# Four edits to a one-core attention and expert kernel: the place of a loop that is not entered, of the state products, of the last counting products and of the first expert's row read

## The chip, the cores and the metric

The kernel runs on one core of a Trainium2 chip. The metric is the device time of one execution in microseconds (us), taken as the median of several runs. A core has five engines that each follow a program of their own and wait for one another through semaphores: PE (matrix products), DVE (vector), ACT (scalar functions), POOL (general, and here the issuer of the indirect transfers) and SP (here the issuer of the plain transfers).

## The reference

Three steps follow one another on 3072 tokens of 384 numbers.

```python
for t in range(768):            # gated linear attention, 4 batches x 8 heads, head size 48
    state = alpha[:, :, t, :, None] * state + k_t (outer) v_t
    y[:, :, t] = q_t @ state
x = y, heads side by side       # 3072 x 384
xn = x / rms(x) * rms_g         # first feed-forward layer, width 1536
x = (silu(xn @ w_gate) * (xn @ w_val)) @ w_out
e_idx = argmax(x @ gate)        # one of 8 experts for each token, width 1024
out[mask_e] = weight * (relu(x[mask_e] @ w1[e]) @ w2[e])
```

## The kernel before, in words

Tokens are handled in 24 tiles of 128 for the attention and in groups of three tiles (384 tokens) for the first layer. Large products are made from operands split into a high and a low part, three products for one.

**Attention.** `stages(t)` gives five steps for a tile t: the scores (tile `ps_s`), a transposition of k (`ps_k`, copied to `kn`), the output (`outp`, tile `ps_y`), the state's new part (`state`, tile `ps_st`: 16 products of `v` and `kn`, 64x48 each) and the transposed, normalised output (`ps_x`). All five take their PSUM tile from one rotating set. The main loop over groups g has 36 slots n in a group; each slot issues nine products of 128x384 of the first layer (tiles `ps_g`, `ps_v`, `ps_o`), and at set counts one attention step is put between two slots. So `ps_y` and `ps_st` of a tile stand in two different slots.

**Routing.** `route_a` and `route_b` of a group find each token's expert. Six small products (tile `ps_r`, with the constants `tri_b` and `ones_b`) count the tokens of each expert ahead of a token; DVE makes positions of them (`rk`, `pos`), and POOL scatters the rows `R` to a DRAM buffer `bucket` that has a region for each expert.

**Experts.** The experts are taken in the order of their counts. `parts` lists the units of work u: u=0 and u=1 are the two halves, 256 rows each, of the leading expert, which is known six groups early or so (`pick_first`); u=2 to 8 are the other seven experts, known only when the last group is counted (`pick_rest`, which also has SP load 21 addresses in all into registers, line 915). `load_rows` reads a unit's rows from `bucket` (tile `er`, queue of SP), `prep_rows` transposes them (`ps_t`, then `x2a` or `x`), `e_h(u, j)` makes a slice of the hidden layer (`ps_h`, then `h` on ACT and DVE), `e_o` multiplies it on (`ps_b`), `e_fin` scales the result and has POOL scatter it to the output (`out_dram`). `load_w1` and `load_w2` read the weights in pieces (tile `st`, queue of SP); ACT, DVE and POOL split them into the two parts.

**Surplus loop.** Rows beyond an expert's place in this scheme would be handled by a loop over `nblk` blocks at the end of the program (lines 1251 to 1323). On these inputs `nblk` is 0, so its body is not run, but each engine has to load the number (line 1223), wait for its own earlier work and jump over it. After it come the closing instructions of the program (line 1353).

**What sets the order.** Each engine runs its instructions strictly in the program's order. That order comes from a scheduler which simulates the kernel and may move what the code writes; where `strict[0]` is set and in `seq(...)` the order as written is kept. The mark `keep_in_program_order` does the same for one instruction.

Of the kernel before, what the change touches and what calls it, by code (L numbers as in the profile page):

```python
# [8 lines left out]
F32 = mybir.dt.float32  # L9
# [36 lines left out]
    'XO': 2,  # L46
    'STRICT': 4,
# [7 lines left out]
def gla_glu_moe_kernel(  # L55
# [16 lines left out]
    nc = tc.nc  # L72
# [771 lines left out]
    att_stream = (st for t in range(GT, NTILE) for st in stages(t))  # L844
# [180 lines left out]
    def e_h(u, j):  # L1025
        p, _, r, n = parts[u]
        xh, xl = x2[u]
        ps = psE.tile([P, r * n], F32, tag="h", name="ps_h", bufs=2)
        mm3(ps, *(w_[:, :, j * P:j * P + P] for w_ in we[p][0:2]), xh, xl)
        hh = act.tile([P, 2, r * n], F32R, tag="xl" if j % 2 else "xh", name="h2")  # L1030
        nc.scalar.activation(hh[:, 0, :], ps, AF.Relu)  # L1031
        nc.vector.scalar_tensor_tensor(out=hh[:, 1, :], in0=ps, scalar=0.0, in1=f(hh[:, 0, :]),  # L1032
                                       op0=ALU.max, op1=ALU.subtract)
        h2[u, j] = hh
# [32 lines left out]
    for g in range(2, NG):  # L1067
# [15 lines left out]
        for n in range(3 * KF):  # L1083
# [14 lines left out]
            if last:  # L1098
# [6 lines left out]
                if n == 30:  # L1105
                    load_rows(0, er0)
                if n >= 33:
                    prep_rows(0, n - 33)
# [21 lines left out]
    route_b(NG - 1)  # L1130
    pick_rest()
# [37 lines left out]

    lag = []  # L1170
# [24 lines left out]
    load_rows(1, ers[1])  # L1195
    load_next(1)
    weight_step()
# [3 lines left out]
    for u in range(U):  # L1201
        for j in range(KF2):
# [10 lines left out]
            elif j > 1 and u < U - 1:  # L1213
                pop_o()
            if u and j == 0 and u + 1 < U:
# [14 lines left out]
        if u >= 1 and u + 1 < U:  # L1230
            while ready or pw:
                weight_step()
            if parts[u + 1][0] + 1 < E:
                addresses(parts[u + 1][0] + 1)
                load_next(parts[u + 1][0] + 1)
    u = U - 1
# [4 lines left out]

    psE.release()
    psM.release()
    xp.release()
    wpool.release()


    with ExitStack() as ov:
        op_ = ov.enter_context(tc.tile_pool(name="op", bufs=1, side="right", reuse_waits="tile"))
        pp = ov.enter_context(tc.tile_pool(name="pp", bufs=2, space=PSUM))  # L1250
        with tc.For_i(0, nblk, 1):
            def sm(nm, w=1, dt=F32):
                return op_.tile([P, w], dt, tag=nm, name=nm)
            V = nc.vector
            ge = sm("ge", E)
            V.tensor_scalar(out=ge, in0=cb, scalar1=obk[:, 0:1], scalar2=None, op0=ALU.is_le)
            ef = sm("ef")
            V.tensor_reduce(out=ef, in_=ge, op=ALU.add, axis=AX.X)
            oh = sm("ohx", E)
            V.tensor_scalar(out=oh, in0=io8[:, 0, :], scalar1=ef[:, 0:1], scalar2=None, op0=ALU.is_equal)  # L1260
            V.tensor_tensor(out=ge, in0=oh, in1=cnt[:, 0, :], op=ALU.mult)
            ne = sm("ne")
            V.tensor_reduce(out=ne, in_=ge, op=ALU.add, axis=AX.X)
            V.tensor_tensor(out=ge, in0=oh, in1=cbx, op=ALU.mult)
            sl = sm("sl")
            V.tensor_reduce(out=sl, in_=ge, op=ALU.add, axis=AX.X)
            V.tensor_tensor(out=sl, in0=obk, in1=sl, op=ALU.subtract)
            V.tensor_tensor(out=ge, in0=oh, in1=capE[:, :, 0], op=ALU.mult)
            ce = sm("ce")
            V.tensor_reduce(out=ce, in_=ge, op=ALU.add, axis=AX.X)  # L1270
            V.scalar_tensor_tensor(out=sl, in0=sl, scalar=float(P), in1=ce, op0=ALU.mult, op1=ALU.add)
            V.tensor_tensor(out=sl, in0=sl, in1=pid[:, 0:1], op=ALU.add)
            rw = sm("rw")
            V.scalar_tensor_tensor(out=rw, in0=ef, scalar=float(REG), in1=sl, op0=ALU.mult, op1=ALU.add)
            ri = sm("ri", 1, I32)
            V.tensor_copy(ri, rw)
            V.tensor_tensor(out=sl, in0=sl, in1=ne, op=ALU.is_lt)
            V.scalar_tensor_tensor(out=rw, in0=sl, scalar=FAR, in1=rw, op0=ALU.mult, op1=ALU.add)
            zi = sm("zi", 1, I32)
            V.tensor_copy(zi, rw)  # L1280
            nc.gpsimd.indirect_dma_start(out=bucket[:, :], out_offset=OFF(ap=zi[:, 0:1], axis=0),
                                         in_=zrow[:, 0, :], in_offset=None,
                                         bounds_check=E * REG - 1, oob_is_err=False)
            r0 = nc.values_load(ri[0:1, 0:1], engines=[mybir.EngineType.SP], min_val=0, max_val=E * REG - P)
            wi = sm("wi", KD + KF2, I32)
            wf = sm("wf", KD + KF2)
            e3 = sm("e3", 2)
            V.tensor_scalar(out=e3[:, 0:1], in0=ef, scalar1=float(DM), scalar2=None, op0=ALU.mult)
            V.tensor_scalar(out=e3[:, 1:2], in0=ef, scalar1=float(F2), scalar2=None, op0=ALU.mult)
            V.tensor_scalar(out=wf[:, 0:KD], in0=pid[:, 1:1 + KD], scalar1=e3[:, 0:1], scalar2=None, op0=ALU.add)  # L1290
            V.tensor_scalar(out=wf[:, KD:], in0=pid[:, 1 + KD:], scalar1=e3[:, 1:2], scalar2=None, op0=ALU.add)
            V.tensor_copy(wi, wf)
            xr = sm("xr", RW)
            nc.sync.dma_start(xr[:, :], bucket[bass.ds(r0, P), :])
            wa = op_.tile([P, KD, F2], F32, tag="wa", name="wa")
            wb = op_.tile([P, KF2, DM], F32, tag="wb", name="wb")
            for i in range(KD):
                nc.gpsimd.indirect_dma_start(out=wa[:, i, :], out_offset=None,
                                             in_=w1.rearrange("e k n -> (e k) n"),
                                             in_offset=OFF(ap=wi[:, i:i + 1], axis=0))  # L1300
            for i in range(KF2):
                nc.gpsimd.indirect_dma_start(out=wb[:, i, :], out_offset=None,
                                             in_=w2.rearrange("e k n -> (e k) n"),
                                             in_offset=OFF(ap=wi[:, KD + i:KD + i + 1], axis=0))
            pt = pp.tile([P, KD, P], F32, tag="pt", name="ptx")
            for i in range(KD):
                nc.tensor.transpose(pt[:, i, :], xr[:, i * P:i * P + P], ident)
            xo = op_.tile([P, KD, P], F32, tag="xo", name="xo")
            V.tensor_copy(xo, pt)
            po = pp.tile([P, DM], F32, tag="po", name="po")  # L1310
            for j in range(KF2):
                ph = pp.tile([P, P], F32, tag="ph", name="ph")
                for i in range(KD):
                    nc.tensor.matmul(ph, lhsT=wa[:, i, j * P:j * P + P], rhs=xo[:, i, :],
                                     start=(i == 0), stop=(i == KD - 1))
                ht = op_.tile([P, P], F32, tag="ht", name="ht", bufs=2)
                nc.scalar.activation(ht, ph, AF.Relu)
# [40 lines left out]
```

## Time and profile before

| what | value |
|---|---|
| median of 3 runs | 868.49 us (866.66 to 868.85) |
| profiled execution, its own time | 865.15 us |
| its span in the trace | 863.4 us |
| PE busy | 840.6 us, 97% |
| DVE, ACT, POOL busy | 57%, 38%, 16% |
| PE's share of the chain that ended last | 79% |
| granted clock of PE over the span | 0.996 |

The profiled execution is one run under the profiler; 1.75 us of its own time lie outside its span. The busy share is a mean over the whole span. It says which engine has the most work, and not whether a given wait costs time: for that the stretches in which PE is not busy have to be looked at one by one.

### The profile page before, as it was taken

How to read it: one execution, taken by the hardware profiler on the slowest of the kernel's cores; microseconds unless marked ns; L12 is line 12 of the kernel's file. 1: busy time of each engine (PE TensorE's matmuls, PEld its weight loads, DVE VectorE, ACT ScalarE, POOL GpSimd, SP SyncE). 2: the span in 40 equal slices, each digit the busy share in tenths (PEclk: the TensorE clock that was granted, in tenths of full speed). 3: DMA queues.
4: the chain of work that ended last, by engine and by line, in shares of the span. 5: the costliest groups of instructions: out<-in, count | busy, mean ns of one | idle time of the engine just before them, and what ended most of it. 6: DMA issues, size and time to landing. Idle time of an engine off the chain costs nothing.

```text
span 863.4 us, 15649 instructions
## 1 busy us (share of the span) xinstructions
PE 840.6 (97%) x6036; PEld 806.6 (93%) x6036; DVE 491.0 (57%) x1111; ACT 324.7 (38%) x705; POOL 142.2 (16%) x204
## 2 busy tenths in 40 slices
PE   7999999999999999999999999999999999999994
PEld 5899989999999999999999999999998999999994
DVE  7998988577765655765655632343534343444320
ACT  2655543333323332333433332333235343345431
POOL 2100000001100100100010010013124242434331
PEclk9999999999999999999999999999999999999998
DMA  9964555852322222222232000041065165256510
GB/s 192 205 164 147 177 128 140 213 138 80 97 60 54 63 49 60 75 74 52 52 88 60 10 29 1 2 130 63 16 203 196 37 210 169 72 165 202 185 39 24
DMA packets 120268, 88.96 MB, mean 103 GB/s; under 512 B 55291, under 2 KB 115324, under 8 KB 120192
## 3 DMA queue, kind: packets, MB, share of 16 engines
q1 hardware_dynamic: 115728, 78.46, 34.5%
q0 software_dynamic: 4464, 9.48, 3.1%
q8 instruction: 48, 0.79, 0.4%
q14 instruction: 28, 0.23, 0.1%
HBM read 72.11 MB, written 16.07 MB: 102 GB/s over the span
## 4 chain that ended last, share of the span: by engine, by line
PE 79%; DVE 7%; issue 5%; DMA 4%; POOL 2%; SPq 1%; ACT 1%; POOLq 0%; DVEq 0%; ACTq 0%
PE ps_o L638 17%; PE ps_v L604 16%; PE ps_g L604 16%; PE ps_b L1047 9%; PE ps_h L604 9%; PE ps_s L425 3%; DMA st<-in_moe_w_dram 3%; PE ps_y L460 2%; PE ps_y L456 2%; PE ps_st L481 1%; SPq L915 1%; PE ps_k L445 1%; PE ps_x L502 1%; PE ps_t L1011 1%; POOL out_dram L1063 1%
## 5 line engine op out<-in xcount | busy, mean ns | idle before, releaser
L615 DVE TENSOR_TENSOR tt<-tt,ps_v 128x384 f32<-128x384 f32 x96 | 52.9, 551 | 119.8 <-PE ps_v L604 116.8
L618 ACT ACTIVATE hh<-tt 128x384 fp32r<-128x384 f32 x96 | 50.3, 524 | 125.2 <-DVE tt L615 119.5
L596 ACT ACTIVATE tt<-ps_g 128x384 f32<-128x384 f32 x96 | 47.1, 490 | 130.4 <-PE ps_g L604 127.3
L624 DVE TENSOR_TENSOR hl<-tt,hh 128x384 fp32r<-128x384 f32 x96 | 54.4, 566 | 27.5 <-ACT hh L618 27.3
L1032 DVE SCALAR_TENSOR_TENSOR h<-ps_h,h 128x256 fp32r<-128x256 f32 (+6 forms) x72 | 38.0, 531 | 54.2 <-ACT h L1031 53.7
L1047 PE MATMUL ps_b<-w2a,h 128*128 128x384 f32 (+2 forms) x336 | 67.4, 339 | 1.5 <-ACT h L1031 1.5
L604 PE MATMUL ps_v<-xh,wvh 128*128 128x384 f32 x192 | 66.8, 348 | 1.9 <-DVE tt L615 1.9
L604 PE MATMUL ps_g<-xh,wgh 128*128 128x384 f32 x192 | 67.9, 353 | 0.1
L638 PE MATMUL ps_o<-woh,hh 128*128 128x400 f32 x192 | 66.6, 355 | 0.4 <-ACT hh L618 0.4
L638 PE MATMUL ps_o<-wol,hh 128*128 128x400 f32 x192 | 66.4, 346 | 0.0
L1047 PE MATMUL ps_b<-w2b,h 128*114 128x384 f32 (+3 forms) x336 | 65.0, 338 | 0.2 <-ACT h L1031 0.2
L604 PE MATMUL ps_g<-xl,wgh 128*128 128x384 f32 x192 | 64.9, 338 | 0.0
L604 PE MATMUL ps_v<-xh,wvl 128*128 128x384 f32 x192 | 64.9, 338 | 0.0
L604 PE MATMUL ps_g<-xh,wgl 128*128 128x384 f32 x192 | 64.8, 338 | 0.0
L604 PE MATMUL ps_v<-xl,wvh 128*128 128x384 f32 x192 | 64.6, 336 | 0.0
L638 PE MATMUL ps_o<-woh,hl 128*128 128x400 f32 x192 | 63.5, 344 | 0.0
L1047 PEld LDWEIGHTS ps_b<-w2a,h 128*128 128x128 f32 (+2 forms) x336 | 57.5, 181 | 2.7 <-ACT h L1031 2.2
L1047 PEld LDWEIGHTS ps_b<-w2b,h 128*114 128x114 f32 (+3 forms) x336 | 57.5, 175 | 2.1 <-ACT h L1031 0.6
L604 PE MATMUL ps_h<-x,w1b 128*128 128x456 f32 (+3 forms) x288 | 58.4, 343 | 0.0
L1031 ACT ACTIVATE h<-ps_h 128x256 fp32r<-128x256 f32 (+6 forms) x72 | 33.4, 468 | 63.3 <-PE ps_h L604 63.1
L604 PE MATMUL ps_h<-x,w1a 128*128 128x256 f32 (+3 forms) x288 | 53.4, 327 | 0.0
L467 POOL TENSOR_SCALAR ss<-ss 128x1 f32<-128x1 f32 x24 | 5.9, 245 | 282.1 <-ACT xn L466 279.3
(284 smaller groups left out, 1966.0 us busy)
## 6 DMA issues: line engine op xcount, KB each, us to landing
st<-in_moe_w_dram SPq DMA_DIRECT2D x64, 384.0 KB, 4.6
bucket<-zero SPq DMA_DIRECT2D x8, 772.0 KB, 6.2
stg<-in_moe_w_gate_dram SPq DMA_DIRECT2D x12, 384.0 KB, 4.1
stg<-in_moe_w_val_dram SPq DMA_DIRECT2D x12, 384.0 KB, 4.2
stg<-in_moe_w_out_dram SPq DMA_DIRECT2D x12, 384.0 KB, 3.7
v<-in_v_dram SPq DMA_DIRECT2D x23, 192.0 KB, 3.0
blk_a<-in_alpha_dram SPq DMA_DIRECT2D x34, 96.0 KB, 2.4
blk_k<-in_k_dram SPq DMA_DIRECT2D x34, 96.0 KB, 2.2
```

The source lines that it names most:

```text
L425: seq(nc.tensor.matmul(ps[hh][:, p, :], lhsT=kT[r, p, :], rhs=qT[r, p, :], start=True, stop=True))
L456: seq(nc.tensor.matmul(ps[:, p * 2 * D:p * 2 * D + 2 * D], lhsT=qT[:, p, :], rhs=S_[:, p, :], start=(p == 0), stop=False, skip_group_check ...
L460: seq(nc.tensor.matmul(ps[u, h * D:h * D + D], lhsT=Pt[h % 2][:, h // 2, u], rhs=vt[t][:, h, :], start=first, stop=True, skip_group_check= ...
L596: nc.scalar.activation(tt, ps, AF.Silu)
L604: seq(nc.tensor.matmul(ps, lhsT=a_[:, kc, :], rhs=b_[:, kc, :], start=(n == 0), stop=(n == 3 * KD - 1)))
L615: nc.vector.tensor_tensor(out=tt, in0=tt, in1=ps, op=ALU.mult)
L618: nc.scalar.activation(hh, tt, AF.Copy)
L624: nc.vector.tensor_tensor(out=hl, in0=tt, in1=f(hh), op=ALU.subtract)
L638: seq(nc.tensor.matmul(obank[s][i], lhsT=a_[:, sl], rhs=weight(b_, j), start=(j == j0 and n == 0), stop=(j == j1 - 1 and n == 2)))
L1031: nc.scalar.activation(hh[:, 0, :], ps, AF.Relu)
L1032: nc.vector.scalar_tensor_tensor(out=hh[:, 1, :], in0=ps, scalar=0.0, in1=f(hh[:, 0, :]), op0=ALU.max, op1=ALU.subtract)
L1047: ins = nc.tensor.matmul(ob2[u][i][0:r], lhsT=hh[:, a_, sl], rhs=we[p][b_][:, j, :], start=(j == 0 and m == 0), stop=(j == KF2 - 1 and m = ...
```

## The change

There are four edits.

1. The surplus loop is put into a function `overflow()`, behind a test `nblk > 0`, and is called ahead of the products of the last unit; it takes the PSUM tiles of `psE` and the place of the pool `xp` instead of pools of its own.
2. From tile 6 on (`MT`) the output's and the state's products are issued in one step of the stream, and the step that held the state's products is empty.
3. `route_b` of the last group, `pick_rest`, and the first loads behind them (`load_rows(1, ...)`, `load_next(1)`, `weight_step`) move from the point behind `e_h(0, 1)` into the loop, to u=0, j=2, and the order as written is kept there.
4. The first expert's rows are read at n=24 instead of n=30 and transposed at n=28 to 30 instead of 33 to 35 of the last group, and `e_h(1, 2)` takes its PSUM tile from another pool.

```diff
     'XO': 2,
+    'MT': 6,
...
-    att_stream = (st for t in range(GT, NTILE) for st in stages(t))
+    def four(t):
+        s_, k_, y_, d_, x_ = stages(t)
+        def yd_():
+            posts = [y_(), d_()]
+            def post():
+                for p in posts:
+                    if p:
+                        p()
+            return post
+        def no_():
+            return None
+        return s_, k_, yd_, no_, x_
+    att_stream = (st for t in range(GT, NTILE) for st in (four if t >= CFG['MT'] else stages)(t))
...
     def e_h(u, j):
-        ps = psE.tile([P, r * n], F32, tag="h", name="ps_h", bufs=2)
+        if (u, j) == (1, 2):
+            ps = psM.tile([P, r * n], F32, tag=order[4], name="ps_h")
+        else:
+            ps = psE.tile([P, r * n], F32, tag="h", name="ps_h", bufs=2)
...
-                if n == 30:
+                if n == 24:
                     load_rows(0, er0)
-                if n >= 33:
-                    prep_rows(0, n - 33)
+                if n >= 28 and n < 28 + 3:
+                    prep_rows(0, n - 28)
...
     e_h(0, 1)
-    route_b(NG - 1)
-    pick_rest()
...
+    def overflow():
+        xp.release()
+        op_ = tc.alloc_tile_pool(name="op", bufs=1, side="right", reuse_waits="tile")
+        with tc.If(nblk > 0):
+            with tc.For_i(0, nblk, 1):
...
+        return op_
...
     lag = [(0, 0), (0, 1)]
-    load_rows(1, ers[1])
-    load_next(1)
-    weight_step()
...
+            if u == 0 and j == 2:
+                strict[0] = True
+                route_b(NG - 1)
+                pick_rest()
+                load_rows(1, ers[1])
+                load_next(1)
+                weight_step()
+            if u == 0 and j == 3:
+                strict[0] = False
...
+    op_ = overflow()
     u = U - 1
     for i in range(parts[u][3]):
         for _, j in lag:
             e_o(u, j, [i])
         e_fin(u, i)
+    op_.release()
     psE.release()
     psM.release()
-    xp.release()
     wpool.release()
-    with ExitStack() as ov:
-        op_ = ov.enter_context(tc.tile_pool(name="op", bufs=1, side="right", reuse_waits="tile"))
-        pp = ov.enter_context(tc.tile_pool(name="pp", bufs=2, space=PSUM))
-        with tc.For_i(0, nblk, 1):
...
```

What this does to the order of instructions is seen in three places. The first is the end of PE's program, here of before: the last `ps_b` products, then the number of blocks and the jump.

```order
L604 MATMUL ps_h<-x_6994,w1b 128x336
L1047 MATMUL ps_b<-w2b,h_9340 112x384 x3
...
L1047 MATMUL ps_b<-w2b,h_9362 112x384 x3
L1047 MATMUL ps_b<-w2b,h_9384 112x384 x3
L1047 MATMUL ps_b<-w2b,h_9406 112x384 x3
L1223 TENSOR_LOAD tab
L1251 COMPARE_AND_BRANCH
L1251 UNCONDITIONAL_BRANCH x2
```

And the same place after the change (lines are numbered anew), where the body of the loop is left out:

```order
L605 MATMUL ps_h<-x_6994,w1b 128x336
L1068 MATMUL ps_b<-w2b,h_9340 112x384 x3
L1068 MATMUL ps_b<-w2b,h_9362 112x384 x3
L1068 MATMUL ps_b<-w2b,h_9384 112x384 x3
L1068 MATMUL ps_b<-w2b,h_9406 112x384 x2
L1330 TENSOR_LOAD tab
L1193 COMPARE_AND_BRANCH
L1194 COMPARE_AND_BRANCH
L1194 UNCONDITIONAL_BRANCH x2
...
L1193 UNCONDITIONAL_BRANCH
L1068 MATMUL ps_b<-w2b,h_9406 112x384
L1068 MATMUL ps_b<-w2b,h_9340 112x384 x3
```

Of the 36 last products 11 stand ahead of the jump and 25 behind it; on POOL the three scatters of the last unit stand behind the jump now as well, and ahead of it before.

The second place is PE's order around one tile's output in the middle of the program, of before: two of the rows `ps_y` (heads in halves), the nine `ps_o` products of a slot, nine `ps_g`, and then the state's.

```order
L456 MATMUL ps_y<-wide_125,qT 128x96 x4
L460 MATMUL ps_y<-v,P_3570 64x48 x8
L460 MATMUL ps_y<-v,P_3572 64x48 x8
L638 MATMUL ps_o<-woh,hh 128x400
...
L604 MATMUL ps_g<-xl,wgh 128x384
L604 MATMUL ps_g<-xh,wgl 128x384
L481 MATMUL ps_st<-v,kn 64x48 x8
L604 MATMUL ps_v<-xh,wvh 128x384
```

The same tile after the change:

```order
L457 MATMUL ps_y<-wide_125,qT 128x96 x4
L461 MATMUL ps_y<-v,P_3570 64x48 x8
L461 MATMUL ps_y<-v,P_3572 64x48 x8
L482 MATMUL ps_st<-v,kn 64x48 x8
L639 MATMUL ps_o<-woh,hh 128x400
L639 MATMUL ps_o<-wol,hh 128x400
```

The row `ps_st` has moved up by 18 products of the first layer, to directly behind `ps_y`; this is so for 13 tiles. One earlier tile has it there in both kernels.

The third place is PE's order where the last group is counted. Before, the six `ps_r` products stand in three places (rows with `tri_b` or `ones_b` alone are their weight loads), with products of the first expert between them:

```order
L1047 MATMUL ps_b<-w2a,h_6972 128x384 x4
L702 LDWEIGHTS tri_b
L702 MATMUL ps_r<-ohb,tri_b 128x8
...
L1047 MATMUL ps_b<-w2a,h_7046 128x384 x3
L705 LDWEIGHTS ones_b
L705 MATMUL ps_r<-ohc,ones_b 128x8
L1047 MATMUL ps_b<-w2a,h_7046 128x384
...
L706 LDWEIGHTS ones_b
L706 MATMUL ps_r<-ohc,ones_b 128x8
L604 MATMUL ps_h<-x2a_6388,w1a_6385 128x256
```

After the change:

```order
L1068 MATMUL ps_b<-w2a,h_7046 128x384 x6
L1068 MATMUL ps_b<-w2a,h_7060 128x384 x6
L703 LDWEIGHTS tri_b
L703 MATMUL ps_r<-ohb,tri_b 128x8
...
L706 LDWEIGHTS ones_b
L706 MATMUL ps_r<-ohc,ones_b 128x8
L707 LDWEIGHTS ones_b
L707 MATMUL ps_r<-ohc,ones_b 128x8
L605 MATMUL ps_h<-x2a_6387,w1a_6385 128x256
```

They stand together now, behind the `ps_b` products of three slices of the hidden layer. Ahead of this place the last `ps_o` products of the first layer have moved down, behind 12 more `ps_h` products; between the last `ps_o` and the transposition of the second unit's rows PE has 54 `ps_h` and 42 `ps_b` products, and 66 and 42 before. On SP, the two weight loads `st_7332` and `st_7336` stand behind 13 and 15 register loads now (counted from the second request for rows on), and behind 16 and 18 before.

## Rows read from the trace of the kernel before

**Rows 1.** Busy time by stretch: window, length, each engine's us, clock, DMA.
```profile
200.00:300.00 100.00, 100.00 (x812) 95.88 (x811) 65.94 (x168) 35.19 (x84) 12.73 (x22) 1.00 0.28 74
835.00:863.40 28.40, 16.39 (x99) 15.98 (x97) 3.16 (x6) 3.43 (x7) 2.83 (x3) 0.87 0.12 32
```

**Rows 2.** What PE waited for, 560 to 680: us in total, times, longest.
```profile
PE ps_b L1047 <- ACT h L1031: 1.7, 4, 1.0
PE ps_t L1011 <- DMA er<-bucket: 1.1, 1, 1.1
```

**Rows 3.** The state's products on PE between 145 and 520, all together.
```profile
L481 PE MATMUL ps_st<-v,kn x208: 222/222/257, 163.7 to 516.2; 128*64 128x48 f32 x104
```

**Rows 4.** Timeline of PE around one tile's state products: start, us, instruction.
```profile
302.18 0.34 PE L604 MATMUL ps_g<-xl,wgh 128*128 128x384 f32 x1
302.35 0.34 PE L604 MATMUL ps_g<-xh,wgl 128*128 128x384 f32 x1
302.62 0.67 PE L481 MATMUL ps_st<-v,kn 128*64 128x48 f32 x16
303.22 0.44 PE L604 MATMUL ps_v<-xh,wvh 128*128 128x384 f32 x1
303.50 0.34 PE L604 MATMUL ps_v<-xl,wvh 128*128 128x384 f32 x1
```

**Rows 5.** The same timeline where they already stand behind the output's products.
```profile
140.81 0.58 PE L460 MATMUL ps_y<-v,P 128*64 128x48 f32 x14
141.22 0.64 PE L481 MATMUL ps_st<-v,kn 128*64 128x48 f32 x16
141.78 0.44 PE L604 MATMUL ps_g<-xh,wghe 128*128 128x384 f32 x1
```

**Rows 6.** Timeline from the last count to the second unit's rows.
```profile
620.87 0.18 DVE L714 TENSOR_TENSOR rk<-ps_r,cnt 128x24 f32<-128x24 f32 x1 [1.20 <-PE ps_r L706]
621.61 0.43 DVE L1032 SCALAR_TENSOR_TENSOR h<-ps_h,h 128x256 fp32r<-128x256 f32 x1
628.78 0.36 SPq L996 DMA_DIRECT2D er<-bucket  x1
632.12 0.84 PE L1011 MATMUL ps_t<-ident,er 128*128 128x128 f32 x6 [1.10 <-DMA er<-bucket]
```

**Rows 7.** Timeline from SP's second rows request to PE's longest wait here.
```profile
631.84 0.53 SPq L996 DMA_DIRECT2D er<-bucket  x1
644.65 0.37 SPq L971 DMA_DIRECT2D st<-in_moe_w_dram  x1
647.74 0.84 ACT L977 ACTIVATE w2b<-st 128x768 fp32r<-128x768 f32 x1 [0.99 <-DMA st<-in_moe_w_dram]
648.91 0.97 PE L1047 MATMUL ps_b<-w2a,h 128*128 128x384 f32 x4 [0.99 <-ACT h L1031]
```

**Rows 8.** Timeline of the end.
```profile
844.93 6.46 PE L1047 MATMUL ps_b<-w2b,h 128*112 128x384 f32 x36
845.13 0.45 ACT L1031 ACTIVATE h<-ps_h 128x336 fp32r<-128x336 f32 x1 [0.94 <-PE ps_h L604]
852.29 0.93 POOL L1063 DMA_INDIRECT out_dram<-ob,ix  x1 [1.10 <-ACT ob L1059]
```

**Rows 9.** The loop's line and its number's: ns min/median/max, first and last start.
```profile
L1251 POOLq EVENT_SEMAPHORE  x16: 17/43/2288, 853.1 to 858.0; - x16
L1251 PEldq COMPARE_BRANCH  x3: 97/179/325, 848.8 to 858.2; - x3
L1251 POOLq INC_SWDGE_SEM  x1: 1224/1224/1224, 855.6 to 855.6; - x1
L1223 ACTq TENSOR_LOAD <-tab x1: 859/859/859, 851.4 to 851.4; - x1
```

**Rows 10.** The closing line, same columns.
```profile
L1353 POOLq DRAIN  x3: 40/103/4327, 858.3 to 863.2; - x3
```

**Rows 11.** The page's instruction queue: packets, MB, share of 16 engines.
```profile
q8 instruction: 48, 0.79, 0.4%
```

More of the change, by code (lines that the diff above doesn't have):

```diff
@@ L1240, in gla_glu_moe_kernel @@
         e_fin(u, i)
+    op_.release()
     psE.release()
     psM.release()
-    xp.release()
     wpool.release()
-    with ExitStack() as ov:
-        op_ = ov.enter_context(tc.tile_pool(name="op", bufs=1, side="right", reuse_waits="tile"))
-        pp = ov.enter_context(tc.tile_pool(name="pp", bufs=2, space=PSUM))
-        with tc.For_i(0, nblk, 1):
[L1252 to L1317, printed above, removed]
-                nc.tensor.matmul(po, lhsT=ht, rhs=wb[:, j, :], start=(j == 0), stop=(j == KF2 - 1))
-            yo = sm("yo", DM)
-            V.tensor_scalar(out=yo, in0=po, scalar1=xr[:, DM:DM + 1], scalar2=None, op0=ALU.mult)
-            ti = sm("ti", 1, I32)
-            V.tensor_copy(ti, xr[:, RW - 1:RW])
-            nc.gpsimd.indirect_dma_start(out=out[:, :], out_offset=OFF(ap=ti[:, 0:1], axis=0),
-                                         in_=yo[:, :], in_offset=None, bounds_check=NT - 1, oob_is_err=False)
-            V.tensor_scalar(out=obk, in0=obk, scalar1=1.0, scalar2=None, op0=ALU.add)
```

74 lines of the change are left out of this document (added).

## The prediction

> **What bounds the kernel now.** The busy time by stretch comes first. From 200 to 300, as in every stretch up to 560, PE is busy for the whole of its window, at clock 1.00 [rows 1]: there a PE product less is time less, and nothing else counts. The second row is the end: of the 28.4 us from 835 on PE has 16.39 us of work, so 12.0 us come after its last product. Then PE's waits between 560 and 680, where the last group hands over to the experts: four waits of `ps_b` for `h` of ACT, 1.7 us, and one of `ps_t` for the rows `er`, 1.1 us [rows 2]. So the time is PE's work, plus some 3 us of waits at that boundary, plus a tail of 12 us without PE. Each edit acts on one of these three. From 680 to 835 nothing that the trace shows is idle on PE and nothing is edited.
>
> **State's products behind the output's.** No product is added or removed; what can change is what it costs PE to go from one form of product to another and back. Where the state's 16 products stand alone, the step into them is 302.62 − 302.35 = 0.27 us against 0.17 between two equal products (302.35 − 302.18), they take 303.22 − 302.62 = 0.60, and the step from the first product behind them to the second is 303.50 − 303.22 = 0.28 against 0.17 [rows 4]. One tile has them directly behind the output's in the kernel before. There they start with no extra step (14 output products in 141.22 − 140.81 = 0.41 us, 0.03 each, and the state's right behind) and take 141.78 − 141.22 = 0.56 [rows 5]; the step out of the small form is paid once for both. So a tile saves 0.10 + 0.11 + 0.04 = 0.25 us. The view of the state's products alone has 208 of them between 163.7 and 516.2 [rows 3], 13 groups of 16, and these are the 13 tiles whose row moves. 13 × 0.25 = 3.3 us, all in the stretches where PE is never idle. The bounds are 0 (the step is paid inside the pair too, which rows 5 speak against) and 13 × 0.30 = 3.9 (the small products go on at 0.033 each). For `kn` and the PSUM tile the products now come about 5 us earlier; I cost a wait for them at nothing, as the tile of rows 5 has none. If that cover is missing it is the rival on the slow side below.
>
> **Last group's counting products together.** The chain here is: `ps_r` on PE, `rk` on DVE at 620.87 and behind it, after a piece of `h` (0.43 us from 621.61), the positions; then three scatters on POOL, their landing, the request `er<-bucket` at 628.78, and `ps_t` at 632.12 after 1.10 us of idle PE [rows 6]. First, when is the last `ps_r` done? By the order before the change, 28 `ps_h` and 10 `ps_b` lie between the last `ps_o` and the last `ps_r`; by the changed order 9 and 18, with 12 `ps_h` more ahead of that `ps_o`, so 21 and 18 in all. At about 0.13 us for a `ps_h` (two thirds of the columns of a 0.17 us product, an estimate) and 0.17 for a `ps_b` that is 8 × 0.17 − 7 × 0.13 = 0.45 later, less about 0.3 for a wait that goes (next part): much the same time as before. Then, by DVE's order after the change, the positions come ahead of that piece of `h`: 0.43 earlier. I take 0.4 us for the scatters, the request and `ps_t`. The bounds: 0.5 later (DVE's routing work starts only behind the later `ps_o`, and holds up `ps_r`) and 1.1 earlier (the whole wait).
>
> **First expert's rows sooner.** The two transpositions and the `ps_h` behind them are ready ahead of the last `ps_o`, so that PE has work at 616 while ACT makes `h`: one of the four waits for `h` goes. The longest of them is 0.99 [rows 7], so the other three are (1.7 − 0.99) / 3 = 0.24 each [rows 2]. Since PE idles at `ps_t` behind it anyway, that alone gives nothing: it only makes the wait at 632 longer. Behind that point it is different. `e_h(1, 2)` has a PSUM tile of its own, so PE has a third slice to work on before the first `ps_b` of u=1: another wait of 0.24 goes, and this one is on the path. The longest wait, 0.99 us at 648.91, is one for `h`, which stood on ACT behind the splitting of a weight piece that began at 647.74 when it landed; SP had requested the piece at 644.65 [rows 7]. Between SP's row request, done at 632.37, and that one lie 18 register loads; (644.65 − 632.37 − 0.6 for the other weight request) / 18 = 0.65 us each. 15 are ahead of it now: 1.9 us earlier, and the row request is 0.4 earlier too. ACT then has the piece well before 647, and the 0.99 goes. Cover and price: the three loads stand behind the weights now and are needed for later units only. The row read itself moves ahead of weight pieces on SP; none of PE's waits in rows 2 is for those weights, so I cost it at nothing; if it made them late, PE would wait at its first `ps_b`. Sum for this and the part above: 0.4 + 0.24 + 0.99 = 1.6 us, between −0.5 (the request 0.5 later and nothing gained behind it) and 2.6 (all the waits of rows 2 but one of 0.24).
>
> **Surplus loop ahead of the last products.** What is removed lies behind the last product. It starts at 844.93 and the 36 of them last 6.46 us, so T = 851.39; the span ends at T + 12.0 [rows 8]. In between: ACT scales the last tile, POOL scatters it from T + 0.90 to T + 1.83, waits up to 2.288 us for it to land (T + 4.05), spends 1.224 us on the count of its software queue, passes the rest of the semaphores and the jump until 858.1 [rows 9], and starts a DRAIN at 858.3 that takes 4.327 us [rows 10]; then 0.8 us of closing steps. In the changed kernel the count, the semaphores and the jump are done ahead of the last scatters. POOL comes to its DRAIN right behind the third scatter, at about T + 2.05. If the DRAIN takes its 4.33 us from there, the end is T + 2.05 + 4.33 + 0.83 = T + 7.2, a gain of 4.8. If the DRAIN was so long only because of the work just ahead of it, the other engines' waits for the landing decide, T + 4.05 + 0.8 + 0.83 = T + 5.7, gain 6.3. If its end is tied to the landing (862.6 is 7.2 us behind it), the end is T + 12.1, gain 0. No row tells these apart; I take the middle one, in which a duration stays what it was.
>
> What is added is a stop of PE in the middle of the last products. PE's jump waits until its last product is through (0.34 long, 0.17 of it normally hidden), then comes a semaphore, and up to two branches of 0.18 to 0.325 us [rows 9]: 0.17 + 0.05 + 0.5, with the first product behind it some 0.9 us. At the low end, branches like the shortest row (0.097) and the number loaded early, it is 0.3. The other engines' loads of the number are covered: ACT's takes 0.859 us [rows 9], its last `h` ends at 845.58 [rows 8], and the first of the three tiles to be scaled is done by PE at about 844.93 + 12 × 0.18 = 847.1. POOL's 1.2 us falls in the 13 us before its first scatter. Net: 4.8 − 0.9 = 3.9 us.
>
> **Rivals.** (a) The DRAIN's end is tied to the landing. For it: nothing else in the trace has a long DRAIN, so 4.327 is no fixed price. Against it: the landing is long over when it starts. Sum: 3.3 + 1.6 − 0.9 = 4.0, so 864.5. (b) The step between forms is paid inside the pair: 3.3 goes, 863.0. Rows 5 speak against it. (c) The jump on PE brings a stop for code. The instruction queue moved 48 packets in 0.4% of 16 engines' span [rows 11], 0.004 × 863.4 × 16 / 48 = 1.15 us for one; two taken jumps would cost 2.3 us more, 862.0. In the trace no engine stops that long at a jump in the row of branches, 0.325 at most; but PE had no work behind its jump there. The Trainium skill, page "Runtime: NRT & Kernel Launch", section "Instruction fetch mechanics", says that a taken branch to a place outside the two code pages in hand stops the engine until the page is fetched; by it this edit would pay such a stop, unless the loop's body is short enough to be in hand. No row here shows one. (d) The change doesn't do what it says at the boundary: the counting products come later by as much as the later `ps_o` push DVE's routing, and the request for the rows follows 1:1. At 1.5 us later the boundary gives nothing: 861.3. (e) On the slow side: the state's products, directly behind the output's, wait for their PSUM tile or for `kn`, and every later product on PE waits with them. With a wait w in each of 13 tiles the sum is 1.6 + 3.9 − 13 w; the kernel gets slower by more than 2.6 us from w = 0.62 us on, and at w = 1 it takes 876.0. Against it: rows 5, and no wait of a state product on PE anywhere in rows 1's full stretch.
>
> **How the numbers follow.** 3.3 + 1.6 + 3.9 = 8.8 us off the profiled execution's 865.15 gives 856.4. Its own time is 3.3 us below the median of the runs shown; against that median, 868.49, the forecast is 859.7. Chances: forecast 0.53, (a) 0.13, (b) 0.08, (c) 0.11, (d) 0.10, (e) 0.05. Likeliest case's own range: 857 to 862. The range reaches down to the better DRAIN and the upper bound at the boundary (859.7 − 1.5 − 1.0 = 857.2, less about 1 for the spread of runs around their median) and up to (a) with the runs' spread, 866. A measurement of this kernel can tell about 0.3%, 2.6 us, from no change: faster holds the forecast and (a) to (d) alone, less the cases in which two of them meet (0.09, "same"); slower is (e).
>
> **What would show it.** State: behind `ps_y` no gap, one step of 0.28 for the pair, PE's work before 560 shorter by about 3 us. Boundary: `er<-bucket` earlier against the last `ps_o`, PE's wait there under 1.1 us, no wait of 1 us for `h` behind it. Tail: a hole of under 1 us among the last `ps_b`, the span ending some 7 us behind the last product with no count of the software queue in between. It is wrong if the DRAIN ends as late behind the landing as before, if the hole in the last products is 2 us or more, or if `ps_st` shows waits.

## The result and the profile after

The changed kernel takes 857.32 us (854.66 to 858.14), the kernel before in the same series 867.58 (865.88 to 868.85); the ratio is 0.9871, with an interval from 0.9842 to 0.9900. It is faster by 10.3 us by the medians; the interval of the ratio goes from 8.7 to 13.7 us. In a second series the ratio was 0.9860 (0.9825 to 0.9895). The forecast was 8.8 us. One run of all, in e11 below, took 911.9 us at a granted clock of 0.85 and is left out of every median and ratio here.

The first trace of the changed kernel has a span of 856.3 us. The busy time by stretch (columns as in [rows 1]) shows a full PE again from 200 on, and a smaller part without PE at the end:

```profile
200.00:300.00 100.00, 100.00 (x824) 96.90 (x823) 66.93 (x167) 34.28 (x82) 14.27 (x22) 1.00 0.28 74
830.00:856.30 26.30, 19.20 (x115) 18.45 (x113) 3.66 (x7) 3.88 (x8) 4.89 (x5) 0.91 0.14 38
```

In the last 26.3 us 7.1 are without PE, and 12.0 were [rows 1]. What PE waited for between 560 and 700, as in [rows 2]:

```profile
PE ps_t L1029 <- DMA er<-bucket: 1.4, 1, 1.4
PE ps_o L639 <- ACT hh L619: 0.6, 1, 0.6
PE ps_b L1068 <- ACT h L1052: 0.2, 1, 0.2
```

Of the four waits for `h`, 1.7 us, one of 0.2 is left; the wait for the rows has grown from 1.1 to 1.4. A tile's state products in the timeline of PE, to be held against [rows 4]:

```profile
322.77 1.14 PE L461 MATMUL ps_y<-v,P 128*64 128x48 f32 x32
323.73 0.64 PE L482 MATMUL ps_st<-v,kn 128*64 128x48 f32 x16
324.30 0.45 PE L639 MATMUL ps_o<-woh,hh 128*128 128x400 f32 x1
324.59 0.34 PE L639 MATMUL ps_o<-wol,hh 128*128 128x400 f32 x1
```

They start behind `ps_y` without the step of 0.27 us into them, and one step out (0.29 us, 324.30 to 324.59) serves both. And the end in the timeline, against [rows 8]:

```profile
842.50 6.85 PE L1068 MATMUL ps_b<-w2b,h 128*112 128x384 f32 x36
...
850.24 0.94 POOL L1084 DMA_INDIRECT out_dram<-ob,ix  x1 [1.10 <-ACT ob L1080]
```

The 36 last products take 6.85 us instead of 6.46: the hole costs 0.39. The last product ends at 849.35, and the span 6.99 behind it. The rows of the jump and of the closing line (columns as in [rows 9]) show where the rest went:

```profile
L1193 POOLq INC_SWDGE_SEM  x1: 1164/1164/1164, 839.5 to 839.5; - x1
L1193 PEldq COMPARE_BRANCH  x1: 368/368/368, 843.8 to 843.8; - x1
...
L1381 POOLq DRAIN  x3: 40/113/5504, 850.0 to 856.1; - x3
```

The count of the software queue starts at 839.5 and takes 1.16 us, ahead of the scatters. PE's jump begins at 843.8, while products issued before it still run. POOL's DRAIN begins at 850.0 and ends 4.33 us behind the last scatter's end (850.0 + 5.50 = 855.5; 850.24 + 0.94 = 851.18). In the kernel before it took 4.327 us from its own start, which lay 5 us behind the last scatter's end [rows 8], [rows 10].

### The profile page after: what moved, and what is told of

It is laid out like the page before. It is cut to its first block, busy times and chain, and to the rows that moved or that the text cites. A ratio compares the mean times of both kernels' runs of the same rounds, so it can differ in the third digit from the quotient of the medians.

```text
span 856.3 us, 15588 instructions
## 1 busy us (share of the span) xinstructions
PE 838.4 (98%) x6036; PEld 807.8 (94%) x6036; DVE 494.4 (58%) x1111; ACT 324.1 (38%) x705; POOL 146.1 (17%) x204
## 4 chain that ended last, share of the span: by engine, by line
PE 80%; DVE 7%; DMA 6%; issue 4%; ACT 1%; POOL 1%; SPq 1%; POOLq 0%; DVEq 0%; ACTq 0%
PE ps_o L639 17%; PE ps_v L605 16%; PE ps_g L605 16%; PE ps_b L1068 10%; PE ps_h L605 9%; DMA st<-in_moe_w_dram 3%; PE ps_s L426 3%; PE ps_y L461 2%; PE ps_y L457 2%; DMA out_dram<-ob,ix 1%; PE ps_st L482 1%; PE ps_k L446 1%; PE ps_t L1029 1%; PE ps_x L503 1%; PE pc L570 1%
## 5 line engine op out<-in xcount | busy, mean ns | idle before, releaser
L468 POOL TENSOR_SCALAR ss<-ss 128x1 f32<-128x1 f32 x24 | 8.2, 340 | 274.0 <-ACT xn L467 271.2
```

## The experiments

All kernels were timed against the kernel before on the same chip, e4 and the second trace of the kernel before with one time each; every one also left one trace. To compare them, each trace is cut at the same products. The columns are: start of the first `ps_o` product; from it to the 97th; from there to the 769th; from there to the 113th `ps_b` product (in the third unit); to the first of the 36 last products; those 36; from the end of the last one to the end of the span. All in us, counted out of the traces. Each label is that of an experiment below; "again" is a second trace of the same kernel. "Boundary" is the stretch in which the last group hands over to the experts.

```
                      1st   to 97th  to 769th  boundary  to last 36   36     tail
before                43.9   75.58   446.46     96.55     182.49     6.46   12.04
before, again         47.2   75.19   446.46     96.18     182.88     6.46   12.01
changed               44.7   77.47   442.20     95.17     182.96     6.85    6.99
changed, again        44.5   74.66   442.20     94.13     182.94     6.83    6.99
e1 state apart        43.9   75.30   446.46     94.38     182.49     6.85    7.01
e2 loop at end        43.9   77.46   442.45     95.60     183.52     6.46   10.38
e3 old boundary       47.4   75.12   442.20     95.41     183.13     6.85    7.01
e4 no last scatter    44.3   75.78   442.20     95.02     182.58     6.85    4.89
e5 counts apart       43.9   75.21   442.20     97.08     183.54     6.85    6.99
e6 rows late          43.8   78.80   442.20     97.36     183.18     6.85    6.99
e9 long body          43.8   78.00   442.20     95.38     183.85    11.20    7.00
e10 boundary alone    44.5   75.91   446.46     94.06     182.88     6.46   11.83
e7 all tiles          47.2   73.26   441.62     94.76     183.48     6.85    7.00
e11 rows earlier      47.4   76.77   442.12     94.38     183.07     6.85    6.99
```

Two things have to be known to read it. Up to 160 us the traces of the kernel before and of the changed kernel have the same working instructions and transfers in the same order on every engine, so what differs between them in the first two columns is a difference between executions. And in some stretches PE was granted half its clock (0.50, 1.2 GHz) for 3.4 us: in the second column in the changed kernel's first trace, e2, e6 and e9, which are its four longest values, and in the boundary in e5 and e6 alone. In e5 it came behind a wait of 2.3 us, in e6 behind one of 1.8 us:

```profile
630.00:633.00 3.00, 3.00 (x16) 3.00 (x16) 0.55 (x2) 0.00 (x0) 0.44 (x1) 0.52 1.06 381
```

```profile
641.00:644.00 3.00, 3.00 (x13) 3.00 (x12) 1.97 (x4) 1.00 (x2) 2.20 (x1) 0.50 0.45 137
```

In e9 equal products follow one another every 0.32 us at 0.50, and every 0.17 to 0.18 at 1.00, so 3.4 us at half clock cost about 1.5 us, an estimate.

**State's products back in a slot of their own (e1).**

```diff
-    'MT': 6,
+    'MT': 99,
```

> The changed kernel with the state's products back in a slot of their own. Theory (the step between the two forms of product is paid once for a pair): 13 tiles cost 0.33 us each again, as the first layer's products drift apart by 4.3 us between 120 and 540 in the two traces; in this run's trace that drift against the changed kernel is back, and the time is about 4.3 us above the changed kernel's, 861 to 862. Rival (the drift comes from another thing, such as the vector engine being less in the way): drift under 1 us, time within 1 us of the changed kernel's. My forecast had 0.25 a tile, 3.3 in all.

Measured: ratio 0.9947 (0.9929 to 0.9966), median 862.83. In the third column the four traces with the state's products apart have 446.46 us, to the hundredth. Of the nine with `MT` at 6 seven have 442.20; e2 has 442.45 and e11 442.12. The timeline of PE in this run has the lone group back:

```profile
302.08 0.34 PE L605 MATMUL ps_g<-xh,wgl 128*128 128x384 f32 x1
302.35 0.67 PE L482 MATMUL ps_st<-v,kn 128*64 128x48 f32 x16
302.95 0.44 PE L605 MATMUL ps_v<-xh,wvh 128*128 128x384 f32 x1
303.24 0.34 PE L605 MATMUL ps_v<-xl,wvh 128*128 128x384 f32 x1
```

0.27 into it, 0.60, 0.29 out of it, as in [rows 4] but for a hundredth. The theory holds: 4.26 us for 13 tiles, 0.33 each.

**Loop behind the last scatters (e2).**

```diff
-    op_ = overflow()
     u = U - 1
...
         e_fin(u, i)
+    op_ = overflow()
```

> The changed kernel with the surplus loop called behind the last scatters. Theory (the count of the software queue, the waits and the jump lie in series behind the last scatter, and POOL's DRAIN takes 4.3 us from the end of POOL's last work): the hole of 0.3 us in the last products goes, the span ends 12.0 us after the last product instead of 6.95, so about 4.7 us above the changed kernel, 862. Rival (the DRAIN's end is set by something that the place of the loop doesn't move): 7 us behind the last product, as in the changed kernel, and time 0.4 below it.

Measured: ratio 0.9909 (0.9889 to 0.9929), median 860.21. The hole is gone (6.46), and the tail is 10.38: longer than 6.99, but not the 12.0 that I expected. The rows of the loop's line and of the closing line:

```profile
L1193 POOLq EVENT_SEMAPHORE  x4: 17/43/2001, 851.1 to 853.3; - x4
...
L1193 POOLq INC_SWDGE_SEM  x1: 1224/1224/1224, 853.4 to 853.4; - x1
...
L1381 POOLq DRAIN  x3: 40/107/4324, 854.6 to 859.5; - x3
```

POOL again waits for the landing, counts its queue, and starts its DRAIN behind that, at 854.6; the DRAIN takes 4.324 us again. But the loop's line has 4 semaphore waits on POOL where it had 16 [rows 9]. This run keeps the test `nblk > 0` and the shared PSUM tiles of the first edit. So of the 5.05 us that the tail lost, 3.4 are the place's and 1.65 belong to these two; that it is the test that spares the waits is likely, but the two were not run apart.

**Third and fourth edit undone (e3).** The moved lines stand where they were, with `n == 30`, `n >= 33` and the old PSUM tile in `e_h`.

> The changed kernel with the third and fourth edits undone: counting products apart, rows read at n=30, the old PSUM tile for the slice. Theory (the boundary gives what the traces show between the last slots of the first layer and the second unit): 1.4 us above the changed kernel, 858.7, with the waits for h at the second unit, 0.24 and 0.99, back. Rival (what is gained there is given back later: the lead of the changed kernel falls from 2.91 to 2.43 us between 680 and 790): only 0.9 above, the lead of the changed kernel over this one falling after 680 too.

Measured: ratio 0.9882 (0.9863 to 0.9901), median 857.87. The times don't tell it from the changed kernel. In its trace the boundary has 95.41 us, in the two of the changed kernel 95.17 and 94.13: one trace is not enough to size this, since two traces of the changed kernel differ by a microsecond here. My expectation of the waits fails: the 0.99 us for `h` is not back. PE's waits for `h` of ACT between 560 and 700 in this run:

```profile
PE ps_b L1065 <- ACT h L1049: 0.5, 2, 0.2
```

The rival (gained there and given back later) is not ruled out either. From the start of the boundary to the last 36 products the nine traces with both edits take 276.9 to 279.2 us, mean 277.85, and the three with neither (this one and the two of the kernel before) 278.5 to 279.1, mean 278.88: 1.0 us, and the groups overlap.

**Last scatter left out (e4).**

```diff
-        e_fin(u, i)
+        e_fin(u, i, i < parts[u][3] - 1)
```

> The changed kernel without its last scatter: the last 112 rows of the last unit's third tile are not written. Theory (DRAIN runs 4.33 us from the end of POOL's last transfer descriptor work): the last of the two scatters left ends 2.1 us earlier, DRAIN ends 4.33 behind it, and the span about 4.9 us behind the last product (6.95 with the third). Rival 1 (DRAIN waits for the transfer's landing plus some time, 2.5 us): the same within 0.3. Rival 2 (DRAIN is a fixed 5.5 us from its start, or ends by the last product): over 6 us.

Measured: one time, 853.3, with the last rows not written. The tail is 4.89 us. The timeline of POOL and the closing line:

```profile
845.55 0.95 POOL L1086 DMA_INDIRECT out_dram<-ob,ix  x1 [1.20 <-DVE ob L1082]
```

```profile
L1383 POOLq DRAIN  x3: 40/113/5436, 845.3 to 851.3; - x3
```

The DRAIN ends at 845.3 + 5.4 = 850.7, 4.25 us behind the end of the last scatter that is left (846.50). It follows the scatter, not the last product. Rival 2 falls. Rival 1 isn't told apart by this run, because the landing moves along. It falls by e2 and the kernel before: there POOL has waited for the landing before the DRAIN starts, and it still takes 4.32 us.

**Changed kernel again, and each half of the boundary undone (e5, e6).** e5 puts back the place of the counting products alone, e6 the lines `n == 30`, `n >= 33` and the PSUM tile alone.

> The changed kernel once more, as the measure for the runs beside it. Theory (the late start and the wait at 118 us in its first trace are differences between executions, set by when the first transfers land, and no work of the edits): the first product of the output weights starts within a microsecond of the 43.9 us of the kernel before, and the lead over the kernel before at the end of the last product is 4 to 6 us instead of 2.0; the state's products lead 4.25 us again. Rival (the edits make the start late): first output product near 44.7 again and the wait at 118 us 2.5 us or more.

> The changed kernel with the third edit alone undone: the counting products and what follows them stand where the kernel before has them. Theory (the holding together brings the request for the second unit's rows about 0.4 us nearer to the last output product): the wait at the second unit's transposition 0.4 us longer, time 0.4 above the changed kernel's, not to be told in the times. Rival (it costs, since the routing starts later): the wait shorter, by up to 0.5.

> The changed kernel with the fourth edit alone undone: first expert's rows at n=30, their transposition at 33 to 35, the old PSUM tile. Theory (it gives the two waits for h of 0.24 and brings the weight requests early): these waits are back in the trace, the boundary between the last slots of the first layer and the third unit gives 0.5 to 1.2 us less than in the changed kernel beside it. Rival (the boundary is set by when weights and rows land, which differs by a microsecond between executions): no difference outside that spread.

Measured: the changed kernel 0.9860 (0.9825 to 0.9895), e5 0.9876 (0.9834 to 0.9919), e6 0.9867 (0.9829 to 0.9906). The times can't be told apart. The changed kernel's second trace starts at 44.5 us, but its wait at 117 us is 1.0 instead of 2.5; the kernel before waits 1.9 and 1.5 there. With the same instructions up to 160 us, the long wait is not the edits'. The second trace leads the kernel before by 6.6 us at the start of the last 36 products, and the first by 2.4. In the boundary's column both e5 and e6 are the longest of all, 97.08 and 97.36. But some 1.5 us of each are the stretch at half clock above; without it they would be about 95.6 and 95.9, an estimate, between the means of the kernels with both edits and with neither (94.76 and 96.05, see e10). The longest wait of PE in e5 between 560 and 700:

```profile
PE ps_t L1029 <- DMA er<-bucket: 2.3, 1, 2.3
```

With the rows read sooner but the counting products apart, PE waits longest for the second unit's rows. The request for these rows shows why. Counted from the start of the boundary, it comes at 61.3 to 62.2 us in the nine traces with both edits, at 62.4 to 62.9 in the three with neither, at 61.8 in e6 (third edit alone) and at 63.3 in e5 (fourth alone). So by these traces it is the third edit that brings the request forward, and the fourth by itself puts it off; e5 and e6 have one trace each.

**Third and fourth edit alone on the kernel before (e10).**

> The kernel before with the third and fourth edits alone. Theory (together they shorten the boundary by 1.0 to 1.6 us): between the first of the last 96 output products and the first waits of the third unit 1 to 2.4 us less than in the kernel before in the same place, time 1.0 to 1.6 below it, ratio near 0.9985. Rival (what the traces show there is a spread between executions, and the edits give nothing): no difference beyond 0.5 us, ratio 1.000.

> The kernel before once more, for a second trace. Theory of the spread: its boundary takes the same time as in the first trace within 0.7 us, and its wait at 117 us differs by some tenths. If it differs by over 1 us at the boundary, no single trace can size the third and fourth edits.

Measured: e10 has a ratio of 0.9977 (0.9958 to 0.9995), median 866.48: faster by 2.0 us, 0.4 to 3.6. The boundary is 94.06 us; the kernel before has 96.55 and, again, 96.18. Over all traces the nine with both edits have 94.06 to 95.60, mean 94.76; the three with neither 95.41 to 96.55, mean 96.05. So the two edits together give some 1.3 us at the boundary, though e3's 95.41 lies below the longest with both; by the start of the last 36 products 1.0 is left (e3). The time of e10 speaks against the rival (nothing), by an interval that stays clear of no change by 0.4 us. The kernel before's two traces differ by 0.4 at the boundary, as expected.

**A loop body 32 times as long (e9).**

```diff
-                for j in range(KF2):
+                for j in [j for _ in range(32) for j in range(KF2)]:
```

> The changed kernel with a loop body 32 times as long in products (about 1000 products on PE that are not run), so that PE's and the scalar engine's jumps go far. Theory (a jump costs PE no fetch of code, as the hole was 0.3 us): hole of 0.48 between two products as before, time within 1 us. Rival (the jump was short enough that its target was in hand; the page's rule of a stop at a far jump): the hole grows by the time of one code packet or more, 1.15 us, and ACT's or POOL's jump may hold the scaling up as well.

Measured: ratio 0.9941 (0.9917 to 0.9966), median 863.39. The body is not run, and yet it costs. My theory falls here, and the rival (c) of the prediction appears. The timeline of PE, the row of its jump, and its clock by stretch:

```profile
843.28 2.09 PE L1068 MATMUL ps_b<-w2b,h 128*112 128x384 f32 x11
848.35 6.13 PE L1068 MATMUL ps_b<-w2b,h 128*112 128x384 f32 x25 [2.98 <-PEq L1193]
```

```profile
L1193 PEldq COMPARE_BRANCH  x1: 3609/3609/3609, 844.6 to 844.6; - x1
```

```profile
847.00:848.00 1.00, 0.00 (x0) 0.00 (x0) 0.00 (x0) 0.00 (x0) 0.00 (x0) 1.00 0.03 8
...
849.00:850.00 1.00, 1.00 (x4) 0.96 (x4) 0.00 (x0) 0.37 (x1) 0.36 (x1) 0.50 0.00 0
850.00:851.00 1.00, 1.00 (x5) 0.95 (x5) 0.00 (x0) 0.00 (x0) 0.59 (x1) 0.50 0.00 0
851.00:852.00 1.00, 1.00 (x5) 0.96 (x4) 0.00 (x0) 0.00 (x0) 0.00 (x0) 0.50 0.52 161
```

The jump takes 3.609 us where it took 0.368, PE stands idle for 2.98, and the granted clock is 0.50 (1.2 GHz) for some three microseconds of the products behind it. The 36 products take 11.20 us instead of 6.85. The instruction queues move four packets from 843 to 850, and two in the changed kernel from 840 to 848. The Trainium skill, page "Runtime: NRT & Kernel Launch", section "Instruction fetch mechanics", says that a taken branch to a place outside the two code pages in hand stops the engine until the page is fetched. This run agrees with the rule: a stop of 2.98 us. The changed kernel shows its other side, a body that is jumped at the price of a hole of 0.39 us. The time rose by 7.2 us against the changed kernel in the same series (856.22); the last products give 4.35 of them, the tail nothing, and where the rest comes from was not looked into.

**Two attempts to go on (e7, e11).** e7 sets `MT` to 3; e11 sets `PREP6`, the slot from which a tile's rows are asked for, from 7 to 4.

> The changed kernel with the state's products behind the output's from tile 3 on instead of 6. Theory (0.33 us for each tile that moves): two more tiles, 0.7 us less where PE is never idle, but these lie ahead of the wait at 117 us, which takes it back: time within 0.5 us of the changed kernel's. Rival (gain kept): 0.7 below, 855.5.

> The changed kernel with the number that sets when the attention rows of a tile are asked for at the start lowered from 7 to 4, so that SP asks for them ahead of one weight piece more. Theory (the wait at 117 us ends with the vector engine, which is held by the rows blk_q landing late): the wait of 1.0 to 2.5 us shrinks by 0.5 or more, the stretch at half clock behind it does not come, and the time is 1 us below the changed kernel's, 855. Rival (other work holds the vector engine there): no change.

Measured: e7 0.9847 (0.9822 to 0.9873), median 855.95; e11 0.9866 (0.9839 to 0.9893), median 856.93. e7 is the fastest by median of all kernels that write every row, but its interval overlaps the changed kernel's. Its trace shows no wait of PE between 100 and 200, and its second column, 73.26, is the shortest; I had expected the wait to take the gain back. Three tiles more have the pair, not two (at 43.4, 65.2 and 77.1 us). With one trace it is not shown that the missing wait is their doing. e11 is a miss. Its waits between 100 and 200:

```profile
PE ps_v L605 <- DVE tt L616: 2.3, 2, 1.6
```

The wait became two, of 2.3 us together, and the time didn't move. That the rows' landing sets this wait is not shown, then.

## Why the prediction was right

The time lies in the range, 0.3 us above the lower end of the likeliest case, and the mechanism of the first two edits is the one described; at the boundary it is only in part. The time came out 2.4 us under the forecast of 859.7: 1.5 are a larger gain, and 0.9 come from the kernel before, which measured 867.58 beside it and not 868.49. By the steps of the prediction:

**State's products.** The 3.3 us were 4.26. The step "0.10 + 0.11 + 0.04 = 0.25 a tile" was too small by 0.08. It missed that the last output product also gives way to the large form: 32 output products take 1.06 us ahead of a large product in the kernel before (322.25 to 323.31 in its timeline, below), and 0.96 ahead of the state's (322.77 to 323.73). That is one more piece of a step that the pair saves.

```profile
322.25 1.14 PE L460 MATMUL ps_y<-v,P 128*64 128x48 f32 x32
323.31 0.45 PE L638 MATMUL ps_o<-woh,hh 128*128 128x400 f32 x1
```

Rows 5, from which I took the sum, show where the pair's products start, not what a lone output group pays. Rivals (b) and (e) fall by the third column and the timeline: no wait, no step inside the pair.

**Counting products and rows sooner.** 1.6 us were forecast and about 1.3 are measured, over many traces. The request `er<-bucket` starts 7.8 us behind the last `ps_r` instead of 8.1 in the first trace. Counted from the start of the boundary it comes 0.9 us earlier in the mean of all traces, where I took 0.4. So rival (d) falls. In the first trace the waits for `h` went, all but one, as forecast. But the reason that I gave for the longest, 0.99 us, is not borne out: in e3 and e6 the weight load stands behind 18 register loads, as in the kernel before, and the longest wait for `h` is 0.2 us there too. The shorter list of loads need not be what removed it. That the wait at `ps_t` would be under 1.1 us was wrong: it is 0.9 to 1.8 in the traces with both edits, since PE comes there earlier. It is the third edit that brings the request forward (e5, e6); how much of the 1.3 us is the fourth's stays open.

**Tail.** 4.8 − 0.9 = 3.9 us were forecast, and 5.05 − 0.39 = 4.7 measured. The middle case for the DRAIN was the right one: 4.33 us, counted from the end of the last scatter, with an end at T + 6.99 where I had T + 7.2. Rival (a) falls. The hole was over-sized, 0.9 us against 0.39: I had the jump wait for the last product ahead of it, but the branch of 0.37 us begins at 843.8, while those products run, and only about 0.3 us of standstill is left. With a hole of 0.39 rival (c) falls for this body; e9 shows it for a longer one. What I put down to the place of the loop alone is to a third the work of the test and the shared tiles (e2).

**The sum.** 4.26 + 1.3 + 4.7 = 10.3 us, or 10.0 with the 1.0 that is left of the boundary's gain. That this meets the difference of the medians, 10.3, to the tenth is luck: its interval is 8.7 to 13.7 us, and in the second series the medians differ by 12.8 (869.03 and 856.22). In the two first traces the spans differ by 7.1 only. The rest lies mainly ahead of the edits' places: a first product 0.9 us later, and 1.9 more up to the 97th `ps_o`, where the changed kernel waited 2.5 us at 118 us, 0.6 longer than the kernel before, and then ran at half clock. In the second trace of the changed kernel the first product is 0.6 later, and the way from it to the 97th 0.9 shorter than in the kernel before; its span is 852.2. Not a step of the prediction, but the reason why one trace each would have misled by 3 us.

## What to carry to other kernels

Where one engine is full, look for the steps between two forms of its instructions and put the groups of one form side by side: here one border less was worth 0.33 us in each tile. Work that each engine has to do once at the end (counts, waits, a jump over a loop that is not entered) can be done ahead of the last real work, where most of it is hidden; the price is a hole in the full engine: 0.39 us for a body of some 35 products, 4.35 for one of some 1000. And a trace's end-to-end difference should be cut at common points before it is explained: here almost three microseconds of it lay ahead of the place of any edit. The granted clock belongs to such a cut: two of the boundaries looked longest mainly because of it.

## What the runs showed of the hardware that I had not expected

- POOL's DRAIN at the end of the program ends 4.25 to 4.33 us behind the end of the last scatter in the ten traces in which nothing else of POOL's lies between them. In the other four (the kernel before twice, e2, e10) POOL waits for the landing and counts its queue first, and the DRAIN takes 4.32 to 4.33 us from its own start. So it takes as long where the landing is over as where it is not.
- A jump over a long body, which is never run, takes 3.609 us on PE instead of 0.368, and the granted clock is 0.50 behind it.
- After a wait of 2.5 us that ended at 118 us in the first trace of the changed kernel the granted clock was 0.50 from 118 to 121, with PE busy; in its second trace, with a wait of 1.0 there, it was not lowered. The rows are two of the first trace and one of the second:

```profile
116.00:118.00 2.00, 0.00 (x0) 0.00 (x0) 2.00 (x5) 0.00 (x0) 0.00 (x0) 0.90 0.46 100
118.00:121.00 3.00, 2.90 (x9) 2.90 (x10) 2.97 (x9) 2.06 (x5) 0.00 (x0) 0.50 0.81 215
```

```profile
118.00:121.00 3.00, 3.00 (x21) 3.00 (x20) 2.97 (x7) 1.31 (x5) 0.00 (x0) 1.00 0.85 212
```

- The start of the first `ps_o` product falls into two groups over the traces, 43.8 to 44.7 and 47.2 to 47.4 us, for the kernel before as for the others. The clock goes with it: in the four traces of the second group (the second of the kernel before, e3, e7, e11) the granted clock is 0.50 for 10.2 us from about 15 us on, and in none of the other ten. The first and the second trace of the kernel before:

```profile
4.00:12.00 8.00, 7.65 (x36) 5.17 (x37) 6.52 (x16) 0.00 (x0) 1.86 (x15) 1.00 1.47 180
16.00:24.00 8.00, 7.75 (x98) 6.02 (x97) 8.00 (x20) 4.64 (x13) 2.00 (x4) 1.00 1.02 236
```

```profile
4.00:12.00 8.00, 6.83 (x36) 4.93 (x37) 6.51 (x16) 0.00 (x0) 1.86 (x15) 1.00 1.47 178
16.00:24.00 8.00, 8.00 (x75) 6.84 (x75) 6.42 (x14) 1.98 (x6) 0.76 (x2) 0.50 1.04 237
```

Ahead of the fall, from 4 to 12 us, PE was without work for 1.17 us in the second trace and for 0.35 in the first. Where that comes from was not looked into.
